# Four-column scaling moved to ScalarE, and GpSimd's value scaling cut in halves, in a chain of attention and two expert layers

## The chip, the cores and the metric

The kernel runs on one core of a Trainium2 chip. A core has five engines that run side by side: TensorE (PE in the profile; its weight loads are PEld) for matrix products, VectorE (DVE), ScalarE (ACT), GpSimd (POOL), and SyncE (SP), which here issues all DMA transfers. Each works through its own queue in order. The metric is the device time of one execution in microseconds, the median over several; lower is better.

## What is computed

```python
# q, k, v: 4 batches x 8 heads x 576 positions x 64
scores = where(block(i) >= block(j), q @ k.T / 8, -1e9)      # blocks of 64 positions
x = softmax(scores) @ v                                      # to 2304 tokens x 512
p = domain_probs / (domain_probs.sum(-1) + 1e-9)             # 2304 x 4
y = sum over e of p[:, e:e+1] * (relu(x @ w1[e]) @ w2[e])    # 4 experts, 512 -> 1024 -> 512
h = y @ w_in                                                 # 512 -> 1024
s = h * softmax(h)
out = (s - mean(s)) / sqrt(var(s) + 1e-6) * g_ln @ w_out     # 1024 -> 512
```

## The kernel before

The 2304 tokens are 18 tiles of 128 rows. Products run in 16-bit pieces: a tensor is scaled by a power of two, its high part is the value rounded to 16 bits, its low part what remains, and three products of the parts stand for one. So nearly every operand is made in two instructions: a high part on ScalarE or GpSimd, then a low part on VectorE that reads it.

The attention goes batch by batch and tile by tile. The values of a batch are five blocks of 128 x 512 (the first batch is key 0; two more blocks, whose key is a tuple, serve the first query block of two batches each). For the second to fourth batch a block is loaded, its squares are summed for the scale, it is loaded again when its turn comes (vraw), and v_split makes its parts: the high part on GpSimd (line 881), the low part on VectorE (line 882). The product of probabilities and values is line 1021; the probabilities come to it transposed, pT, through a DMA.

When the attention of a tile is ready, finish() closes it in three steps: rows (divide by the sums), scale (sum of squares, from which scale_bits on VectorE computes a power of two, inv, and its reciprocal s), and split: the high part on ScalarE (line 1074), the low part on VectorE (line 1075), a transposing DMA to xT, which the expert layers read, and the tile's four expert probabilities pn multiplied by inv into pt, 128 x 4 numbers (line 1079).

coef_of reads pt on VectorE and multiplies in the scales of the weights: for one tile at a time where an expert's result opens the accumulator (line 454, used on ScalarE at line 417), and for a whole part of the tiles at once else (line 460, used by line 422). Tiles 0 to 5 are the first part, 6 to 17 the second.

The expert layers are units that are mixed in between the steps of the attention: hidden units (line 375 for the products, 385 and 386 for the parts of the result) and output units (line 397). Tiles 0 to 5 go through the first experts while the attention of the others runs. When the attention ends, t_steps and s_steps prepare sums of parts of x and of the weights for the next stage, which needs fewer products (line 629). Weights w_in and w_out come as 64-bit words and are narrowed on VectorE (lines 287 to 310) in between.

The start is emitted in an order written out by hand; there SP's queue is held to the order of emission. Else the program is built with a scheduler that plays a simulated timeline and picks, for each engine, among what is ready by priority; results that TensorE waits for are given a higher one. So an engine's order may differ from the order in the code.

Of the kernel before, what the change touches and what calls it, by code (L numbers as in the profile page):

```python
# [14 lines left out]
AF = mybir.ActivationFunctionType  # L15
ALU = mybir.AluOpType
# [47 lines left out]
def tile_kernel(  # L64
# [38 lines left out]
    vec, act, gp, sync = nc.vector, nc.scalar, nc.gpsimd, InOrder(nc.sync)  # L103
# [18 lines left out]
    pn = cp.tile([128, NTILE, E], F32, name="pn")  # L122
    pt = cp.tile([128, NTILE, E], F32, name="pt")
# [4 lines left out]
    def squares(x, out, junk=None):  # L128

        if junk is None:  # L130
            junk = jp.tile([128, 1024], BF16, tag="junk", name="junk")[:, :x.shape[1]]
        return act.activation(out=junk, in_=x, func=AF.Square, accum_out=out)

    def scale_bits(T, bits, s, inv):

        vec.tensor_scalar(
            out=inv.bitcast(I32), in0=T.bitcast(I32), scalar1=24, scalar2=23,
            op0=ALU.logical_shift_right, op1=ALU.logical_shift_left,
        )
        vec.tensor_scalar(  # L140
            out=inv, in0=inv, scalar1=2.0 ** (64 - bits), scalar2=2.0 ** -75, op0=ALU.mult, op1=ALU.max
        )
        vec.reciprocal(out=s, in_=inv)
# [197 lines left out]
    def xtile(d, t, name):  # L341
        g, c = group(t)
        if g not in d:
            n = GROUPS[g[0]][g[1]][1]
            d[g] = xps[g[0]].tile([128, 2 * KD, 128 * n], F16, tag=f"xT{g[1]}", name=name)
        return d[g][:, :, c:c + 128]
# [397 lines left out]
    class Attention:  # L744
# [132 lines left out]
        def v_split(self, key, j):  # L877
            r = self.raws["v", key, j].pop(0)
            t = self.vp.tile([128, 2, 512], F16, tag="v", name="v")
            s = self.vSc[key]  # L880
            gp.tensor_scalar(out=t[:, 0], in0=r, scalar1=s, scalar2=1.0, op0=ALU.mult, op1=ALU.mult)
            vec.scalar_tensor_tensor(out=t[:, 1], in0=r, scalar=s, in1=t[:, 0], op0=ALU.mult, op1=ALU.subtract)
            self.vS[key, j] = t

# [160 lines left out]
        def finish(self, t):  # L1045

            b, i = TILES[t]
            inv = sp.tile([128, 1], F32, tag="xi", name="xi")
            xf = self.fp.tile([128, NH, HD], F32, tag="xf", name="xf")
            x = xf.rearrange("p h d -> p (h d)")  # L1050
            xh = self.fp.tile([128, 2, 512], F16, tag="xh", name="xh")
            s = sp.tile([128, 1], F32, tag="xs", name="xs")

            def rows():
                ps, sums = self.xps.pop(t), self.sums.pop(t)
                rs = sp.tile([128, NH, 1], F32, tag="rs", name="rs")
                vec.tensor_scalar(
                    out=rs[:, :, 0], in0=sums, scalar1=1e-9 * 2.0 ** PBITS, scalar2=self.vSc[("z", b) if i == 0 else b],
                    op0=ALU.add, op1=ALU.mult,
                )  # L1060
                ri = sp.tile([128, NH, 1], F32, tag="ri", name="ri")
                vec.reciprocal(out=ri, in_=rs)
                vec.tensor_tensor(
                    out=xf, in0=ps.rearrange("p (h d) -> p h d", h=NH), in1=ri.to_broadcast([128, NH, HD]),
                    op=ALU.mult,
                )

            def scale():
                T = sp.tile([128, 1], F32, tag="xt", name="xt")
                squares(x, T, xh[:, 1].bitcast(BF16))  # L1070
                scale_bits(T, 4, s, inv)

            def split():
                act.activation(out=xh[:, 0], in_=x, func=AF.Copy, scale=s)
                vec.scalar_tensor_tensor(
                    out=xh[:, 1], in0=x, scalar=s, in1=xh[:, 0], op0=ALU.mult, op1=ALU.subtract
                )
                sync.dma_start_transpose(out=xtile(xT, t, "xT"), in_=xh.rearrange("p a f -> p (a f)"))
                vec.tensor_scalar_mul(pt[:, t, :], pn[:, t, :], inv)

            return [rows, scale, split]

# [297 lines left out]
    while at1.more:  # L1380
        t, u, cost = moe[-1] if moe else (-1, None, 0)
        ok = t is None or t in ready and len(bg) <= n1
        if not ok or tdv <= tpe + 2.0:
            flush()
            at1.step()
            a, c = at1.cost()
# [233 lines left out]
```

## Time and profile before

| what | value |
|---|---|
| time, median of 3 runs | 1090.99 us (1089.95 to 1091.23) |
| profiled execution, its time | 1090.29 us |
| its span, first to last instruction | 1088.5 us |
| mean granted clock of TensorE, as a share of full | 0.997 |
| TensorE busy | 1041.5 us, 96% of the span |
| VectorE busy | 776.3 us, 71% |
| ScalarE busy | 511.1 us, 47% |
| GpSimd busy | 208.1 us, 19%, all of it before 430 us |
| chain that ended last, by engine | TensorE 84%, DMA 6%, VectorE 4%, GpSimd 3%, ScalarE 1% |

The table is from one execution recorded by the hardware profiler. Busy is the time in which an engine had an instruction under way. The chain that ended last is followed back from the last instruction, at each step to what released it. In the rows below, a window gives its stretch, its length, and for each engine the busy time with the number of instructions in brackets; a timeline gives the start and the duration in us, and in square brackets how long the engine stood idle before and what ended it; a group gives the busy time and the mean of one in ns. An average over the span says little by itself: the kernel has stages with different limits, and the rows below are by stage.

### The profile page before, as it was taken

The page shows a single profiled execution, that of the slowest core. Times are in us where ns is not written, and L with a number is a line of the kernel's source. Part 1 is how long each engine was busy: PE and PEld are TensorE (multiplying, and loading weights), DVE is VectorE, ACT ScalarE, POOL GpSimd, SP SyncE. Part 2 cuts the span into 40 slices and gives each one's busy share as a digit, 9 for nine tenths or more (in the row PEclk, how much of TensorE's full clock was granted, in tenths as well). Part 3 has the DMA queues.
Part 4 walks back from the last instruction along what each step waited for, and adds up shares of the span by engine and source line. Part 5 has one row for each costly group of instructions (what it writes and reads, how often), then busy time and mean ns, then how long its engine had stood idle before and what let it go on. Part 6 is the DMA issues. An engine that isn't in the chain of part 4 may idle for free.

```text
span 1088.5 us, 20680 instructions
## 1 busy us (share of the span) xinstructions
PE 1041.5 (96%) x8088; PEld 657.0 (60%) x8088; DVE 776.3 (71%) x1758; ACT 511.1 (47%) x1108; POOL 208.1 (19%) x280
## 2 busy tenths in 40 slices
PE   4679899999999999999899999999999999999998
PEld 4556666656655655655476777776766674444444
DVE  6879677748767765545786557665879558999883
ACT  5757578546755454532353334231446353323322
POOL 4967733534237311000000000000000000000000
PEclk9989999999999999999999999999999999999999
DMA  9978997566677865235331211330346312435233
GB/s 295 277 175 167 241 201 189 143 173 172 158 178 174 186 112 129 56 90 157 122 97 51 77 47 55 117 136 30 98 145 167 77 24 36 88 88 106 60 87 87
DMA packets 225745, 137.96 MB, mean 127 GB/s; under 512 B 184560, under 2 KB 193008, under 8 KB 225648
## 3 DMA queue, kind: packets, MB, share of 16 engines
q1 hardware_dynamic: 225648, 136.65, 50.3%
q8 instruction: 63, 1.03, 0.4%
q14 instruction: 34, 0.28, 0.1%
HBM read 79.47 MB, written 12.06 MB: 84 GB/s over the span
## 4 chain that ended last, share of the span: by engine, by line
PE 84%; DMA 6%; DVE 4%; POOL 3%; ACT 1%; issue 1%; SPq 0%; DVEq 0%; ACTq 0%; POOLq 0%
PE ops L397 31%; PE hps L629 14%; PE hps L375 14%; PE o L1536 9%; PE h L1470 9%; PE pv L1021 3%; DMA pT<-hl 3%; PE sps L920 2%; PE sps L923 2%; DMA xT<-xh 1%; POOL ks L800 1%; DMA raw<-in_w_dram 1%; DMA x2T<-xh 1%; DMA near<-in_kT_dram 1%; DMA vraw<-in_vC_dram 1%
## 5 line engine op out<-in xcount | busy, mean ns | idle before, releaser
L397 PE MATMUL ops<-wt,hch 128*128 128x512 f16 x1728 | 393.1, 379 | 2.4 <-DVE wt L238 1.4
L397 PEld LDWEIGHTS <-hch 128*128 128x128 f16 x1728 | 166.1, 98 | 187.4 <-issue 6.7
L375 PE MATMUL hps<-xT,wt 128*128 128x384 f16 (+1 forms) x1536 | 216.1, 290 | 6.3 <-DVE hch L386 3.9
L375 PEld LDWEIGHTS <-wt 128*128 128x128 f16 x1536 | 126.5, 100 | 64.4 <-issue 6.1
L979 ACT ACTIVATE p<-sps,nm 128x320 f32<-128x320 f32 (+3 forms) x120 | 70.1, 587 | 85.1 <-DVE nm L939 75.4
L993 DVE TENSOR_TENSOR hl<-p,hl 128x320 f16<-128x320 f32 (+3 forms) x120 | 75.6, 650 | 37.3 <-ACT hl L992 37.2
L629 PEld LDWEIGHTS <-S 128*128 128x128 f16 x1152 | 96.0, 98 | 3.0 <-issue 0.9
L1536 PE MATMUL o<-wt,lt 128*128 128x512 f16 (+1 forms) x456 | 95.6, 368 | 0.0
L1470 PE MATMUL h<-wt,x2T 128*128 128x512 f16 x432 | 95.5, 379 | 0.0
L238 DVE SCALAR_TENSOR_TENSOR wt<-stage,ws,wt 128x1024 f16<-128x1024 f32 (+1 forms) x64 | 82.9, 1304 | 7.4 <-ACT wt L235 4.3
L422 DVE SCALAR_TENSOR_TENSOR acc<-ops,coef,acc 128x512 f32<-128x512 f32 x54 | 40.4, 748 | 66.4 <-PE ops L397 66.3
L920 PE MATMUL sps<-ks,qhi 128*128 128x288 f32 (+3 forms) x160 | 69.1, 433 | 10.7 <-DVE hl L993 7.5
L629 PE MATMUL hps<-T,S 128*128 128x192 f16 x864 | 76.3, 246 | 0.0
L629 PEld LDWEIGHTS <-wt 128*128 128x128 f16 x864 | 72.8, 98 | 5.8
L642 ACT ACTIVATE stu<-hps 128x384 f32<-128x384 f32 x72 | 34.6, 482 | 86.5 <-PE hps L629 86.3
L1536 PEld LDWEIGHTS <-lt 128*128 128x128 f16 x456 | 44.6, 98 | 48.9
L1470 PEld LDWEIGHTS <-x2T 128*128 128x128 f16 x432 | 42.3, 98 | 51.0
L386 DVE SCALAR_TENSOR_TENSOR hch<-hps,hch 128x384 f16<-128x384 f32 (+1 forms) x98 | 52.8, 540 | 21.9 <-ACT hch L385 21.8
L647 ACT ACTIVATE hch<-stc 128x384 f16<-128x384 f32 x72 | 37.4, 521 | 63.5 <-DVE stc L655 63.2
L385 ACT ACTIVATE hch<-hps 128x384 f16<-128x384 f32 (+1 forms) x98 | 46.9, 481 | 39.5 <-PE hps L375 39.4
L1021 PE MATMUL pv<-v,pT 128*128 128x64 f16 x1392 | 56.6, 196 | 8.9 <-DMA pT<-hl 8.8
L1021 PEld LDWEIGHTS <-pT 128*128 128x128 f16 x1392 | 51.6, 100 | 20.5 <-DMA pT<-hl 10.8
(163 smaller groups left out, 1534.6 us busy)
## 6 DMA issues: line engine op xcount, KB each, us to landing
stage<-in_w_dram SPq DMA_DIRECT2D x50, 512.0 KB, 5.9
raw<-in_qT_dram SPq DMA_DIRECT2D x34, 256.0 KB, 3.1
vraw<-in_vC_dram SPq DMA_DIRECT2D x30, 256.0 KB, 3.2
raw<-in_kT_dram SPq DMA_DIRECT2D x24, 288.0 KB, 3.5
raw<-in_w_dram SPq DMA_DIRECT2D x24, 256.0 KB, 4.1
raw<-in_w_in_dram SPq DMA_DIRECT2D x8, 512.0 KB, 4.7
raw<-in_w_out_dram SPq DMA_DIRECT2D x8, 512.0 KB, 4.2
stage<-wf SPq DMA_DIRECT2D x8, 512.0 KB, 6.6
```

The source lines that it names most:

```text
L238: stage["last"] = vec.scalar_tensor_tensor(out=lo, in0=r, scalar=stage[key, "s"], in1=hi, op0=ALU.mult, op1=ALU.subtract)
L375: pe.matmul(ps[:, j * n:j * n + n], w[:, a, kk, f * 128:(f + 1) * 128], x[:, b * KD + kk, c0:c0 + n], start=(m == 0), stop=(m == 3 * KD - 1),)
L385: marks["A"] = nc.scalar.activation(out=h[:, 0, :n], in_=ps[:, :n], func=AF.Relu)
L386: marks["D"] = nc.vector.scalar_tensor_tensor(out=h[:, 1, :n], in0=ps[:, :n], scalar=0.0, in1=h[:, 0, :n], op0=ALU.max, op1=ALU.subtract)
L397: pe.matmul(ps, hch[f][:, a, o0:o0 + 128], w[:, b, f, :], start=(m == 0), stop=(m == 3 * KF - 1))
L629: i = pe.matmul(ps[x][:, jj * HT:jj * HT + HT], lhs(a, kk, jj), rhs(b, kk), start=start, stop=(m == 5), skip_group_check=not first or jj > 0,)
L920: pe.matmul(o, q, rhs, start=True, stop=False)
L979: act.activation(out=src if direct else dst, in_=src, func=AF.Exp, bias=nm[:, j + x:j + x + 1], scale=SCALE, accum_out=sums[:, h:h + 1],)
L993: anc["D"] = vec.tensor_tensor(out=lo, in0=pf, in1=hi, op=ALU.subtract)
L1021: pe.matmul(o, tt[:, a * nch + c, :], v[:, bb, hs], start=(m == 0), stop=(m == total - 1))
L1470: pe.matmul(ps[:, half], x[:, a * KD + kk, c:c + 128], w[:, b, kk, half * 512:half * 512 + 512], start=(m == 0), stop=(m == 3 * KD - 1),)
L1536: pe.matmul(ps, tt[:, x * KF + f], w[:, y, f, c], start=(m == 0), stop=(m == 3 * KF - 1))
```

## The change

In finish(), the multiplication of the four probabilities by inv moves from VectorE to ScalarE, as a copying activation with inv as its scale; its place in the emitted order stays, behind the tile's transposing DMA. In v_split(), GpSimd's high part of a value block is made by two instructions of 256 columns in place of one of 512, for the batches after the first; the first batch and the two blocks with tuple keys keep the one instruction. VectorE's low part stays one instruction of 512 columns.

```diff
@@ v_split
             s = self.vSc[key]
-            gp.tensor_scalar(out=t[:, 0], in0=r, scalar1=s, scalar2=1.0, op0=ALU.mult, op1=ALU.mult)
+            for c in [slice(0, 512)] if isinstance(key, tuple) or key == 0 else [slice(0, 256), slice(256, 512)]:
+                gp.tensor_scalar(out=t[:, 0, c], in0=r[:, c], scalar1=s, scalar2=1.0, op0=ALU.mult, op1=ALU.mult)
             vec.scalar_tensor_tensor(out=t[:, 1], in0=r, scalar=s, in1=t[:, 0], op0=ALU.mult, op1=ALU.subtract)
@@ finish, split
                 sync.dma_start_transpose(out=xtile(xT, t, "xT"), in_=xh.rearrange("p a f -> p (a f)"))
-                vec.tensor_scalar_mul(pt[:, t, :], pn[:, t, :], inv)
+                act.activation(out=pt[:, t, :], in_=pn[:, t, :], func=AF.Copy, scale=inv)
```

## Rows read from the trace of the kernel before

**Rows 1.** Windows: PE, PEld, DVE, ACT, POOL busy us, clock, DMA share, GB/s.
```profile
0.00:165.00 165.00, 126.14 (x1444) 100.02 (x1444) 127.34 (x293) 109.06 (x298) 108.49 (x138) 0.98 0.94 227
165.00:486.00 321.00, 320.60 (x2564) 190.45 (x2564) 213.58 (x453) 184.86 (x429) 99.58 (x142) 1.00 0.62 144
486.00:523.00 37.00, 33.12 (x216) 18.58 (x215) 22.34 (x51) 11.95 (x23) 0.00 (x0) 1.00 0.51 156
```

**Rows 2.** Waits of PE from 0 to 165 us: total us, times, longest.
```profile
PE pv L1021 <- DMA pT<-hl: 8.8, 6, 2.3
...
PE hps L375 <- DMA xT<-xh: 2.3, 2, 1.9
```

**Rows 3.** Waits of PE from 486 to 523 us.
```profile
PE hps L375 <- DVE hch L386: 3.9, 1, 3.9
```

**Rows 4.** Line 1079: ns min/median/max, first and last start, forms.
```profile
L1079 DVE TENSOR_SCALAR pt<-pn,xi x18: 203/243/729, 37.1 to 493.4; 128x4 f32<-128x4 f32 x18
```

**Rows 5.** Groups of DVE by form: busy us, mean ns, idle before.
```profile
L1079 DVE TENSOR_SCALAR pt<-pn,xi 128x4 f32<-128x4 f32 x18 | 6.7, 372 | 0.0
```

**Rows 6.** Timeline of DVE from 64 us: start, duration, instruction, idle before.
```profile
70.33 0.69 DVE L1079 TENSOR_SCALAR pt<-pn,xi 128x4 f32<-128x4 f32 x1
...
71.72 0.75 DVE L1075 SCALAR_TENSOR_TENSOR xh<-xf,xs,xh 128x512 f16<-128x512 f32 x1 [0.39 <-ACT xh L1074]
```

**Rows 7.** Timeline of POOL from 66 us.
```profile
70.01 0.99 POOL L800 TENSOR_TENSOR ks<-raw,ks 64x384 fp32r<-64x384 f32 x1
```

**Rows 8.** Timeline of DVE from 128 us.
```profile
141.85 0.36 DVE L1079 TENSOR_SCALAR pt<-pn,xi 128x4 f32<-128x4 f32 x1
...
144.15 1.17 DVE L882 SCALAR_TENSOR_TENSOR v<-vraw,vs,v 128x512 f16<-128x512 f32 x1 [0.82 <-POOL v L881]
...
145.43 0.74 DVE L1075 SCALAR_TENSOR_TENSOR xh<-xf,xs,xh 128x512 f16<-128x512 f32 x1
...
152.94 0.49 DVE L993 TENSOR_TENSOR hl<-p,hl 128x320 f16<-128x320 f32 x1 [0.36 <-ACT hl L992]
```

**Rows 9.** Timeline of SP's queue from 100 us.
```profile
114.91 7.10 SPq L94 DMA_TRANSPOSE pT<-hl  x1
```

**Rows 10.** Windows of 20 us, columns as in rows 1.
```profile
80.00:100.00 20.00, 20.00 (x284) 15.62 (x282) 17.55 (x39) 16.40 (x38) 11.86 (x16) 1.00 0.85 184
```

**Rows 11.** Timeline of DVE from 30 us.
```profile
37.11 0.21 DVE L1079 TENSOR_SCALAR pt<-pn,xi 128x4 f32<-128x4 f32 x1
...
51.10 0.27 DVE L1079 TENSOR_SCALAR pt<-pn,xi 128x4 f32<-128x4 f32 x1
```

**Rows 12.** Groups of ACT by form: busy us, mean ns, idle before.
```profile
L1538 ACT ACTIVATE o2s<-o,osc 128x512 f32<-128x512 f32 x17 | 11.6, 684 | 32.4 <-PE o L1536 22.3 <-issue 10.1
...
L1538 ACT ACTIVATE o2s<-o,osc 128x256 f32<-128x256 f32 x2 | 0.9, 474 | 4.0 <-PE o L1536 4.0
```

**Rows 13.** Timeline of all engines from 486 us.
```profile
489.93 0.49 ACT L385 ACTIVATE hch<-hps 128x384 f16<-128x384 f32 x1 [2.33 <-PE hps L375]
...
493.02 0.72 ACT L1074 ACTIVATE xh<-xf,xs 128x512 f16<-128x512 f32 x1 [0.65 <-DVE xs L143]
...
493.36 0.22 DVE L1079 TENSOR_SCALAR pt<-pn,xi 128x4 f32<-128x4 f32 x1
...
493.61 0.69 DVE L460 TENSOR_SCALAR coef<-pt,iw 128x12 f32<-128x12 f32 x3
...
494.21 0.75 DVE L1075 SCALAR_TENSOR_TENSOR xh<-xf,xs,xh 128x512 f16<-128x512 f32 x1
```

**Rows 14.** Line 881's instructions, columns as in rows 4.
```profile
L881 POOL TENSOR_SCALAR v<-vraw,vs x15: 687/692/1652, 134.9 to 372.0; 128x512 f16<-128x512 f32 x15
```

**Rows 15.** Line 798's instructions, columns as in rows 4.
```profile
L798 POOL TENSOR_SCALAR qhi<-raw x62: 397/404/1367, 11.8 to 427.7; 128x256 fp32r<-128x256 f32 x56, 128x512 fp32r<-128x512 f32 x6
```

**Rows 16.** Timeline of SP's queue from 134 us.
```profile
143.41 2.33 SPq L94 DMA_TRANSPOSE pT<-hl  x1
...
146.46 1.23 SPq L94 DMA_TRANSPOSE xT<-xh  x1
```

## The prediction

> **What bounds the kernel now.** First the page's busy times, as in the table above: TensorE has an instruction under way for 96% of the span. Only where it has none, or where it does its work slower, can a change to the other engines show. The windows by stage say where that is [rows 1]: from 165 to 486 us TensorE is busy for 320.60 of 321, at a granted clock of 1.00. A microsecond saved on VectorE or lost on GpSimd there changes nothing, because TensorE always has another matrix product to go on with. Idle are 165 - 126.14 = 38.9 us in the first 165 us, where the attention of the first tiles cannot yet feed it, and 37 - 33.12 = 3.9 us between 486 and 523 us, where the attention ends and the next stage begins. (From 523 us on neither edit has an instruction.) Of the waits of TensorE in the first stretch two bear on this change: 8.8 us for the transposed probabilities pT, and 2.3 us for the transposed tiles xT [rows 2]. In the second it is one wait of 3.9 us, for VectorE's line 386 [rows 3]. So the question is what the two edits do in those two stretches.
>
> **What leaves VectorE.** Line 1079 runs eighteen times, 203 ns at the shortest, 243 in the middle, 729 at the longest, the first at 37.1 and the last at 493.4 us [rows 4]; the group of them takes 6.7 us, 372 ns in the mean [rows 5]. Four numbers in each row can't take 729 ns by themselves. The one at 70.33 lasts 0.69 us and so ends at 71.02 [rows 6]; GpSimd's product from 70.01 lasts 0.99 us and ends at 71.00 [rows 7]. The VectorE instruction stood until GpSimd's had finished. [...] Eleven of the eighteen run after 165 us, where TensorE doesn't idle, but for the last. Of the seven before, the one at 70.33 is followed by 0.39 us in which VectorE waits for ScalarE's line 1074 in any case [rows 6], so its 0.69 us are swallowed. That at 141.85 is followed by a wait of 0.82 us for GpSimd's line 881 [rows 8]. Around the one at 110.79 the queue of SP is the late one: its transposes from 114.91 hold it for 7.10 us [rows 9], and what VectorE would give earlier stands in line there. The one at 93.02 lies in a stretch where TensorE was busy throughout [rows 10], and that at 151.44 is followed by another wait of VectorE for ScalarE [rows 8]. Two remain, that at 37.11 (0.21 us) and that at 51.10 (0.27 us) [rows 11], in rows of VectorE work without a gap. Upper bound of the gain 0.5 us, lower bound nothing, if the transposes later take it back; I take 0.2.
>
> **What comes to ScalarE.** The trace has no activation on four columns. The nearest rows are line 1538's, 684 ns for 512 columns and 474 for 256 [rows 12]: 0.82 ns a column, and 684 - 508 x 0.82 = 267 ns for four. Eighteen of them are at most 4.8 us on an engine that is idle for half of the span. Each comes behind line 1074 of its tile, so its operands are there and it waits for nothing itself. Queued behind it are exponentials and high parts of the next step. On a path to TensorE before 165 us that costs between nothing and 0.27 us, once; I take 0.1. [...]
>
> **The wait that it adds.** Lines 454 and 460 read pt on VectorE, and used to follow line 1079 on the same engine. Now they need a signal from ScalarE. For all but one tile there are many microseconds between. The exception is the last tile: pt at 493.36, at once three coefficients of line 460 (0.69 us for the three), then line 1075 at 494.21, and from that the transpose that the next stage waits for; line 1074 of this tile lies at 493.02 and lasts 0.72 us [rows 13]. With pt on ScalarE it is done at about 493.74 + 0.27 = 494.0. If the coefficients stay in front of line 1075, they end at 494.0 + 0.69 = 494.7 and line 1075 is up to 0.5 us later; TensorE's wait of 3.9 us [rows 3] grows by it. If the scheduler puts them behind it, which they allow (their first use is a stage later), line 1075 starts at 493.8, 0.4 us earlier. Bounds -0.4 and +0.5. I take -0.2, the nearer to the second order, since pt is then the operand that comes last.
>
> **The halves.** Line 881 takes 687 ns at the shortest for 512 columns [rows 14]. The nearest row for 256 is line 798's 397 to 404 ns [rows 15]: two halves are 0.80 us, 0.11 us more than one whole, and at the very most, if a half took as long as the whole, 0.69 us more; line 798's row, the same operation at that width, is the near one. Fifteen of them are 1.7 to 10.4 us on GpSimd. From 165 to 486 us it is busy for 99.58 of 321 us [rows 1], so the ten of them that lie there cost nothing. The five of the second batch lie between 134 and 146 us. There the path is: vraw lands, line 881, line 882 of VectorE at 144.15 behind a wait of 0.82 us for it, line 1075 at 145.43 [rows 8], the transpose at 146.46 [rows 16], and TensorE waits 1.9 us for that xT [rows 2]. Line 882 needs both halves. So +0.1 us, at most 0.7; nothing if its place is taken by other work. What the halves could give is a shorter stand for a VectorE instruction behind GpSimd, half of 0.69 us at a time; no VectorE instruction of line 1079's kind is seen standing behind line 881 in front of an idle TensorE, so I put it at nothing and at 0.3 us as the bound.
>
> **The sum.** -0.2 + 0.1 - 0.2 + 0.1 = -0.2 us; with all the bounds at one end -0.5 - 0.4 - 0.3 = -1.2, at the other 0.27 + 0.5 + 0.7 = +1.5. The profiled execution took 1090.29 us, with 1.8 us around its span; the median of the runs is 1090.99, 0.7 above it, and the same difference goes on that: 1090.8, between 1089.8 and 1092.5. A measurement of this kernel tells about 0.2%, 2.2 us, from no change, so that is the same time.
>
> **Rivals.** The order of each engine comes from a scheduler that plays a timeline, so moving eighteen instructions and adding fifteen can turn the order of others round wherever two were ready together.
> First, faster. At 143 us line 1075's operands had been there since ScalarE ended line 1074, and it stood behind line 882, which waited. If the halves, ready later, let line 1075 go ahead, its transpose is no longer late: by 0.6 us if SP still issues the pT transpose of 143.41 first (it holds the queue for 2.33 us), by the whole 1.9 us of TensorE's wait if it doesn't [rows 2, 16]. Together with 0.4 us at the hand-over and the upper bound of 0.5 us for VectorE's relief that is -2.8 us: 1088.2. For it: 38.9 us of idle time, in a stretch where VectorE is busy for 127.34 of 165 us [rows 1]. Against it: most of the seven are swallowed. It decides from 2.2 us on.
> Second, slower: the coefficients' wait. If the scheduler puts pt of the last tile not straight behind line 1074 but behind an activation that waits for TensorE, as line 385 does for 2.33 us at 489.93 [rows 13], VectorE stands at line 460 with line 1075 behind it, and the wait of 3.9 us becomes 6.2: 1090.99 + 2.3 = 1093.3. It decides as soon as pt comes more than 2.2 us behind line 1074. Against it: pt is ready at the same time as line 1074.
> Third, slower: the transposes. They are TensorE's largest wait in the first stretch, 8.8 us in six waits [rows 2], on one queue with the loads. If the order on that queue changes for the worse, one more wait of the size of the longest, 2.3 us, comes in, or two: 1093.3 to 1095.6.
> That the halves or the move don't do what they say is part of the forecast: it is the same time.
>
> **Chances.** The sum as worked out, same time: 0.46. Faster by turned order and relief: 0.32. The coefficients' wait 0.09, the transposes 0.13: slower 0.22. The range goes from 1086.0 (the first rival twice as large) to 1094.5 (the third, between one and two waits), and leaves out about 2 in 10; the likeliest case's own range is 1089.8 to 1092.5.
>
> **What would show it.** Eighteen activations of line 1079 at 0.2 to 0.3 us on ScalarE; thirty instructions of line 881 on loaded values at about 0.4 us; VectorE's busy time some 6 us lower before 494 us; TensorE as full from 165 to 486 us as now, and 38 to 40 us of idle time before that. The step on the hand-over is read at the last line 1075: before 494.21, counted from its line 1074, or after. Wrong I would be if TensorE's idle time in the first 165 us moves by more than 2 us, or its wait near 520 us by more than one.

## The result and the profile after

The changed kernel takes 1096.49 us (median of 8 runs, 1093.15 to 1099.91), the kernel before beside it 1089.65 (8 runs, 1086.23 to 1091.23): a ratio of 1.0064, with a 95% interval of 1.0046 to 1.0082. By the ratio that is 7.0 us slower, above the range of the forecast. The profiled execution of the changed kernel has a span of 1095.0 us, against 1088.5.

First the windows of the changed kernel; the columns are those of [rows 1]. Its source has one line more, so from line 882 on its lines count one higher: its 882 and 1080 are the edited lines 881 and 1079, its 1075 is ScalarE's line 1074 and its 1076 VectorE's line 1075. The prose below goes by the numbers of the kernel before; the lines of a trace have those of their own kernel, and the code cut of r11 and some of the recorded expectations those of the changed one.

```profile
0.00:165.00 165.00, 124.18 (x1407) 100.93 (x1408) 124.49 (x284) 107.38 (x299) 111.23 (x139) 0.96 0.90 223
165.00:486.00 321.00, 317.94 (x2559) 188.22 (x2559) 206.67 (x436) 186.49 (x438) 104.95 (x156) 1.00 0.63 144
486.00:523.00 37.00, 36.55 (x232) 20.27 (x230) 21.59 (x48) 12.46 (x26) 0.00 (x0) 1.00 0.57 166
```

TensorE idles for 165 - 124.18 = 40.8 us in the first stage, 2.0 more than before, and part of what it does there is done at a lower granted clock (0.96 against 0.98). The new thing is in the second row: 321 - 317.94 = 3.1 us without work where it had 0.4 [rows 1]. The third row looks better only because everything comes some 6 us later, and the wait before the next stage has moved past 523 us.

A count of TensorE's progress says where the time goes. It is the start of the matmul of sps (the scores) with n others of sps before it, worked out from the traces (us); the last three columns are experiments told below.

```
   n    before     after      r10      r12      r13
 140    108.72    108.09   107.64   108.67   106.03
 180    130.44    132.72   130.02   132.51   127.86
 220    164.46    168.64   164.38   168.13   165.18
 260    212.78    218.57   214.22   216.08   214.52
 380    348.65    355.14   352.05   351.84   350.75
 495    477.76    484.22   482.97   481.32   480.67
```

At 108 us the changed kernel is 0.6 us ahead. At 130 it is 2.3 behind, at 165 us 4.2, at 213 us 5.8 and at 349 us 6.5, and that stays. The waits of TensorE from 0 to 165 us, against [rows 2]:

```profile
PE pv L1022 <- DMA pT<-hl: 5.9, 3, 3.7
...
PE hps L375 <- DMA xT<-xh: 2.2, 2, 1.6
...
PE pv L1022 <- POOL qlo L800: 1.8, 1, 1.8
```

The transposed probabilities are waited for three times in place of six, 5.9 us in all in place of 8.8, but once for 3.7 us in place of 2.3 at most. The timeline of TensorE shows that place. Before:

```profile
124.08 1.05 PE L1021 MATMUL pv<-v,pT 128*128 128x64 f16 x30 [0.84 <-DMA pT<-hl]
...
129.24 1.05 PE L1021 MATMUL pv<-v,pT 128*128 128x64 f16 x30 [1.89 <-DMA pT<-hl]
...
134.10 1.05 PE L1021 MATMUL pv<-v,pT 128*128 128x64 f16 x30 [0.93 <-DMA pT<-hl]
```

And in the changed kernel:

```profile
123.35 1.04 PE L1022 MATMUL pv<-v,pT 128*128 128x64 f16 x30
128.04 1.78 PE L1022 MATMUL pv<-v,pT 128*128 128x64 f16 x30 [3.65 <-DMA pT<-hl]
129.63 0.51 PE L921 MATMUL sps<-ks,qhi 128*128 128x192 f32 x1
```

Two groups of pv now stand back to back in TensorE's queue, and the second waits 3.65 us with all the sps and hps work behind it that used to lie between them. Behind the wait the same 30 matmuls take 1.78 us and not 1.05. The windows of 10 us (length, TensorE's busy time and instructions, granted clock, DMA share, GB/s) show why, and show it once more behind the waits at 150 us:

```profile
120.00:130.00 10.00, 6.34 (x82) 0.84 1.12 226
130.00:140.00 10.00, 10.00 (x136) 0.82 0.81 183
150.00:160.00 10.00, 7.41 (x95) 0.83 0.92 235
```

Counted from windows of 2 us, the profiled execution of the changed kernel has four stretches at half clock up to its last matmul (a granted clock of 0.50 by windows of 0.5 us, near 74, 130, 156 and 528 us), 17.0 us together, the one of before a single stretch of 6.8 us near 74 us. The mean granted clock of the runs is 0.993 against 0.997.

Now the two edits' own instructions, against [rows 4, 14] (ns min/median/max, first and last start, forms):

```profile
L1080 ACT ACTIVATE pt<-pn,xi x18: 281/296/310, 37.8 to 498.7; 128x4 f32<-128x4 f32 x18
...
L882 POOL TENSOR_SCALAR v<-vraw,vs x30: 475/528/1497, 137.6 to 379.4; 128x256 f16<-128x256 f32 x30
```

Two halves take 1.06 us by the median, where the whole took 0.69. And ScalarE's timeline shows that pt does not stand behind the activation of its tile (line 1074), as in the source, but in front of it:

```profile
144.30 0.30 ACT L1080 ACTIVATE pt<-pn,xi 128x4 f32<-128x4 f32 x1 [2.58 <-DVE xi L140]
...
145.62 0.71 ACT L1075 ACTIVATE xh<-xf,xs 128x512 f16<-128x512 f32 x1
```

ScalarE waits there 2.58 us for the tile's xi; over the eighteen it is 9.6 us in five waits. So the scheduler has turned the order of the engines. Against the kernel before, 262 of VectorE's 1,740 instructions that both have, 148 of ScalarE's 847, 53 of SyncE's 389 and 1,840 of TensorE's 8,072 stand at another place of their queue.

### The profile page after: what moved, and what is told of

The parts are those of the page before. It is cut to its first block, busy times and chain, and to the rows that moved or that the text cites. A ratio compares the mean times of both kernels' runs of the same rounds, so it can differ in the third digit from the quotient of the medians.

```text
span 1095.0 us, 20688 instructions
## 1 busy us (share of the span) xinstructions
PE 1044.8 (95%) x8088; PEld 660.4 (60%) x8088; DVE 770.8 (70%) x1740; ACT 515.0 (47%) x1126; POOL 216.2 (20%) x295
## 4 chain that ended last, share of the span: by engine, by line
PE 82%; DMA 6%; POOL 5%; DVE 4%; issue 2%; ACT 1%; SPq 1%; DVEq 0%; ACTq 0%; POOLq 0%
PE ops L397 31%; PE hps L629 14%; PE hps L375 13%; PE o L1537 9%; PE h L1471 9%; PE pv L1022 3%; DMA pT<-hl 2%; PE sps L921 2%; PE sps L924 1%; POOL v L882 1%; DMA xT<-xh 1%; POOL ks L800 1%; POOL qlo L800 1%; DVE hl L994 1%; SPq L94 1%
## 5 line engine op out<-in xcount | busy, mean ns | idle before, releaser
L375 PE MATMUL hps<-xT,wt 128*128 128x384 f16 (+1 forms) x1536 | 218.7, 293 | 4.7 <-DVE hch L386 2.4
L375 PEld LDWEIGHTS <-wt 128*128 128x128 f16 x1536 | 129.3, 102 | 63.6 <-issue 7.9
L629 PEld LDWEIGHTS <-wt 128*128 128x128 f16 x864 | 73.2, 98 | 6.1 <-issue 0.3
```

Source lines behind the costliest of these rows:

```text
L375: pe.matmul(ps[:, j * n:j * n + n], w[:, a, kk, f * 128:(f + 1) * 128], x[:, b * KD + kk, c0:c0 + n], start=(m == 0), stop=(m == 3 * KD - 1),)
L629: i = pe.matmul(ps[x][:, jj * HT:jj * HT + HT], lhs(a, kk, jj), rhs(b, kk), start=start, stop=(m == 5), skip_group_check=not first or jj > 0,)
```

## The experiments

Three theories stood at the start. A: the new order is what costs. B: the halves cost, on the way of the values into pv. C: pt on ScalarE costs. A fourth, D, came up with the half-clock stretches: the clock costs.

Most runs hold four engines to a given order; GpSimd's order is left to the scheduler. Every instruction is recorded as the source makes it, and the kernel's own helper `after`, which orders two instructions of one engine without a semaphore, chains them:

```diff
+def hold(logs, after):
+    for key, order in PIN.items():          # TensorE, VectorE, ScalarE, SyncE
+        log = logs[key]
+        for x, y in zip(order, order[1:]):
+            after(log[y], log[x])
```

PIN holds the order read from the kernel before ("the old order") or from the changed one ("the new order"). No run here holds the kernel before, unedited, to its own old order; that holding costs little by itself is read from r8, r15 and r16 below, which are held to it and stand within 0.4 us of the kernel before. Each ratio is to runs of the kernel before on the same chip beside them (medians 1089.4 to 1091.6 us); microseconds are the ratio's excess times 1090.

**Order against work.** First both edits in the old order, and the old instructions in the new order.

```diff
-PIN = (none: the scheduler's order)
+PIN = the old order     # r1: lines 881 and 1079 edited
+PIN = the new order     # r2: neither line edited
```

> Both edits, with each engine held to the order of instructions that the kernel before had (each activation of line 1080 right behind its tile's line 1075, as the source has it). Theory A, the order: the 6.8 us come from the order in which the scheduler puts the instructions of VectorE, ScalarE, SyncE and TensorE once the edits are in; then this run stands at 0.0 to +1.5 us against the kernel before (ratio up to 1.0014). Theory B, the halves' own price: two halves take 1.06 us against 0.69, fifteen times, on the values' way into pv of the second batch; then the run stands at +3 to +6 us whatever the order. Theory C, ScalarE's new work: 18 activations of 0.28 us make ScalarE late for what follows; then +2 to +5 us here too.

> The kernel before's own instructions (whole line 881, line 1079 on VectorE) with each engine held to the order that the changed kernel has. Theory A, the order: +4 to +7 us against the kernel before (1094 to 1097 us), with half-clock stretches at about 127 and 154 us as in the changed kernel. Theories B and C: -0.5 to +1.5 us, since neither the halves nor ScalarE's 18 activations are in it.

Measured: r1 1.0036 (1.0022 to 1.0051), +3.9 us; r2 1.0053 (1.0040 to 1.0065), +5.8 us. The order alone, with nothing of the change in it, costs most of what the change costs: theory A holds. But the work in the old order isn't free either, against A's expectation for r1, and the two don't add up (9.7 for 7.0).

**Each edit alone**, first in the scheduler's own order (r3, r4), then in the old one (r5, r6), and both in the old order with pt in front of line 1074 (r7).

```diff
# r3, r6: line 1079 alone
-                vec.tensor_scalar_mul(pt[:, t, :], pn[:, t, :], inv)
+                act.activation(out=pt[:, t, :], in_=pn[:, t, :], func=AF.Copy, scale=inv)
# r4, r5: line 881 alone
-            gp.tensor_scalar(out=t[:, 0], in0=r, ...)
+            for c in ...:
+                gp.tensor_scalar(out=t[:, 0, c], in0=r[:, c], ...)
```

> Only line 1079 on ScalarE, the order left to the scheduler. Theory A, the order: 41 of SyncE's 389 and 116 of ScalarE's 847 instructions change places, so a loss of +1 to +6 us is possible without any halves, and its place in the span is where the waits of pv on pT move. Theory B, the halves' price: 0.0 +- 1 us. Theory C, ScalarE's new work: +3 to +6 us.

> Only line 881 in two halves from the second batch on, the order left to the scheduler (76 of VectorE's and 16 of SyncE's instructions change places). Theory B, the halves' price: +3 to +6 us, with VectorE's line 883 waiting for the halves of 144 to 147 us. Theory A: between 0 and +3 us, the smaller part of the loss, since fewer instructions change places than with line 1079 moved. Theory C: 0.0 +- 1 us.

> Only line 881 in two halves, with VectorE, ScalarE, SyncE and TensorE held to the order of the kernel before. Both edits in this order gave +3.9 us. Theory B, the halves' own price on the values' way into pv: +2 to +4 us here. Theory C, ScalarE's 18 small activations: 0.0 +- 1 us here. The run with the halves alone in the scheduler's own order gave +0.1 us, which speaks for the second.

> Only line 1079 on ScalarE, each activation right behind its tile's line 1074, and the engines held to the order of the kernel before. Theory C, ScalarE's work: an activation of 0.28 us in a row of work that TensorE waits for; +2 to +4 us, with TensorE's waits on p, qhi, hch or hl grown and the VectorE time of 3.9 us that it frees of no use. Theory A, the order alone: 0.0 +- 1 us. Theory B: 0.0 +- 1 us.

> Both edits, held to the order before as in the run with +3.9 us, except that each activation of line 1080 now stands in front of its tile's line 1075, as the changed kernel's own order has it. If ScalarE standing in front of line 1075 for the tile's xi is what costs, this run is 1 to 3 us above that one (+5 to +7 us against before). If the place does not matter, +3 to +5 us, the same as with the activation behind.

Measured: r3 1.0027 (1.0014 to 1.0040), +2.9 us; r4 1.0001 (0.9989 to 1.0012), +0.1; r5 1.0016 (0.9998 to 1.0035), +1.7; r6 1.0031 (1.0016 to 1.0046), +3.4; r7 1.0035 (1.0017 to 1.0054), +3.8. The halves cost nothing that can be told in the one order, and between -0.2 and +3.8 us in the other: theory B is at most a smaller part. Line 1079 on ScalarE costs in either. Its place in front of line 1074 or behind makes no difference in the old order. Of VectorE's waits in r3, one bears on what follows:

```profile
DVE c L454 <- ACT pt L1079: 0.5, 2, 0.4
```

**What of line 1079 costs.** r8 leaves it out, r9 makes each activation twice, both in the old order.

```diff
# r8
-                vec.tensor_scalar_mul(pt[:, t, :], pn[:, t, :], inv)
# ... and lines 454 and 460 read pn in place of pt
# r9
-                vec.tensor_scalar_mul(pt[:, t, :], pn[:, t, :], inv)
+                for _ in range(2):
+                    act.activation(out=pt[:, t, :], in_=pn[:, t, :], func=AF.Copy, scale=inv)
```

> The kernel before in its own order with line 1079 left out on both engines: the coefficients read the probabilities without the row scale (lines 454 and 460 take pn in place of pt). It leaves out that product, so its output is not the reference's. With line 1079 on ScalarE in this order the kernel stood at +3.4 us. Theory C, the 18 activations on ScalarE cost it: -0.5 to +0.8 us here. Rival, VectorE running 3.9 us freer shifts its evictions and so TensorE's waits and its clock: +2 to +4 us here too.

> As the run with line 1079 on ScalarE in the order before (+3.4 us), with each of the 18 activations made twice. Theory C: the price doubles, +5 to +8 us. If the second costs nothing more (+2.5 to +4.5 us), what costs is not ScalarE's time but that VectorE or a wait has shifted.

Measured: r8 0.9997 (0.9984 to 1.0009), -0.3 us; r9 1.0040 (1.0028 to 1.0052), +4.4. VectorE without the eighteen instructions is neither faster nor slower, and twice the time on ScalarE costs about a microsecond more, not another 3.4. So it is hardly the 0.3 us of an activation. That points to something that the first one brings and the second doesn't double, such as a wait. The waits of VectorE from 0 to 165 us in r6 begin with one that the kernel before doesn't have:

```profile
DVE c L454 <- ACT pt L1079: 7.0, 4, 2.5
```

The same in r9:

```profile
DVE c L454 <- ACT pt L1080: 8.4, 4, 2.8
```

Line 454 makes the first expert's coefficient of a tile, in the middle of the attention. VectorE's timeline in the kernel before, around the fifth tile:

```profile
110.79 0.73 DVE L1079 TENSOR_SCALAR pt<-pn,xi 128x4 f32<-128x4 f32 x1
111.55 0.27 DVE L454 TENSOR_SCALAR c<-pt,iw 128x1 f32<-128x1 f32 x1
111.74 0.15 DVE L871 COPY vt<-vtp 128x1 f32<-128x1 f32 x1
```

The coefficient follows its pt at once. In r6 the same place is this, on VectorE:

```profile
109.31 0.16 DVE L143 RECIPROCAL xs<-xi 128x1 f32<-128x1 f32 x1
111.98 0.27 DVE L454 TENSOR_SCALAR c<-pt,iw 128x1 f32<-128x1 f32 x1 [2.51 <-ACT pt L1079]
112.17 0.15 DVE L871 COPY vt<-vtp 128x1 f32<-128x1 f32 x1
```

on ScalarE:

```profile
111.05 0.72 ACT L1074 ACTIVATE xh<-xf,xs 128x512 f16<-128x512 f32 x1
111.66 0.29 ACT L1079 ACTIVATE pt<-pn,xi 128x4 f32<-128x4 f32 x1
```

and on TensorE:

```profile
112.38 1.03 PE L1021 MATMUL pv<-v,pT 128*128 128x64 f16 x30 [0.77 <-DVE vt L871]
```

VectorE has the scale at 109.5 us. Then it stands 2.51 us, because ScalarE has four other activations to do first and reaches pt at 111.66; behind line 454 in VectorE's queue stands vt, and for that TensorE waits. Yet this pv is not later than in the kernel before:

```profile
112.95 1.04 PE L1021 MATMUL pv<-v,pT 128*128 128x64 f16 x30
```

So the line above shows a way to TensorE, but not the 3.4 us. In r3, in the scheduler's own order, line 454 waits 0.5 us in all; what r3 loses is not this wait. The three runs that follow test the wait of line 454: pt on ScalarE for tiles 0 to 6 alone (r14) or 7 to 17 alone (r15), and for all of them with line 454 freed of it (r16), all in the old order.

```diff
# r14: t < 7, r15: t >= 7
+                if t < 7:
+                    act.activation(out=pt[:, t, :], in_=pn[:, t, :], func=AF.Copy, scale=inv)
+                else:
                     vec.tensor_scalar_mul(pt[:, t, :], pn[:, t, :], inv)
# r16: line 1079 on ScalarE as in r6, and line 454
-                out=c, in0=pt[:, t, e:e + 1], scalar1=c1, scalar2=c2, ...
+                out=c, in0=pn[:, t, e:e + 1], scalar1=c1, scalar2=c2, ...
```

> The order before; line 1079 on ScalarE for tiles 0 to 6 alone (those of the first 165 us), on VectorE for the others. All 18 on ScalarE gave +3.4 us, none at all -0.3 us, each of them twice +4.4 us. If ScalarE is late only where TensorE waits for chains through p, hl and pT, that is in the first 165 us: +2.5 to +4 us here. If every tile costs its share: +1.0 to +1.6 us (7 of 18).

> The order before; line 1079 on ScalarE for tiles 7 to 17 alone, after 165 us, where TensorE is full. If ScalarE is late only in the first 165 us: -0.5 to +0.8 us. If every tile costs its share: +1.8 to +2.4 us (11 of 18).

> The order before and line 1079 on ScalarE for all 18 tiles, as in the run with +3.4 us, except that line 454 (the first expert's coefficient, tile by tile in the attention stage) reads the probabilities without the row scale and so waits for nothing of ScalarE's. It leaves out that scale in those coefficients, so its output is not the reference's. In the run with +3.4 us VectorE stood 7.0 us in four waits of line 454 on pt. If these waits are the cause: -0.5 to +1.0 us. If ScalarE's own time is: +2.5 to +4.5 us still.

Measured: r14 1.0032 (1.0018 to 1.0046), +3.5 us; r15 1.0004 (0.9989 to 1.0019), +0.4; r16 1.0003 (0.9984 to 1.0023), +0.3. In r16 the eighteen activations are all there and VectorE's line 454 waits for nothing:

```profile
109.35 0.25 DVE L454 TENSOR_SCALAR c<-pn,iw 128x1 f32<-128x1 f32 x1
109.89 0.16 DVE L871 COPY vt<-vtp 128x1 f32<-128x1 f32 x1 [0.29 <-PE vtp L869]
```

Five runs in the old order have line 454 waiting for pt (r1, r6, r7, r9, r14: 4.6 to 8.4 us in four waits); they stand at +3.4 to +4.4 us. Three don't (r8, r15, r16); they stand at -0.3 to +0.4. Two with the halves and without the wait (r5, and r17 below) stand at +1.7. So theory C holds, but through line 454, which now needs a result of ScalarE, and not as ScalarE's time.

One rival is not ruled out. GpSimd's order was left to the scheduler, and by the traces it turned in just the five runs with the wait, at 12 to 27 of 280 places (two halves counted as one); in r5, r8, r12, r15, r16 and r17 it is that of the kernel before, in r2, r10, r11 and r13 that of the changed one. GpSimd in the kernel before:

```profile
121.03 1.92 POOL L800 TENSOR_TENSOR qlo<-raw,qhi 128x256 fp32r<-128x256 f32 x2
122.93 0.42 POOL L798 TENSOR_SCALAR ks<-raw 128x288 fp32r<-128x288 f32 x1
```

and in r6:

```profile
121.08 1.33 POOL L798 TENSOR_SCALAR ks<-raw 128x288 fp32r<-128x288 f32 x2
122.38 1.42 POOL L800 TENSOR_TENSOR qlo<-raw,qhi 128x256 fp32r<-128x256 f32 x2
```

Freeing line 454 (r16) took away both, so the runs do not separate VectorE's wait from GpSimd's turned order. The clock may have a part as well, by an estimate: over the 118 runs of the kernel before that stand beside the experiments, 0.001 less of mean granted clock goes with some 0.7 us more. The five runs' means are 0.992 to 0.995, against 0.996 to 0.997 for the three and 0.997 for the kernel before; that would be 1 to 3 of their 3.4 to 4.4 us. It is a correlation, and no run tests it. How the 3.4 us come together isn't shown: r6's profiled execution was its fastest, 1090.65 us.

**Where the order costs.** r11 is the changed kernel with the second of the two pv groups put 45 matmuls later in TensorE's queue. r10 leaves the order and fills the two waits with matmuls that pv then writes over.

```diff
# r11: TensorE's part of PIN, instructions by their number in the source's order
-  ..., 893 to 922 (pv of tile 5, pair 2), 45 matmuls of lines 921 to 926, 397 and 375, ...
+  ..., 45 matmuls of lines 921 to 926, 397 and 375, 893 to 922 (pv of tile 5, pair 2), ...
# r10: in front of the group's first matmul, line 1021
+            for _ in range({(5, 2): 60, (7, 0): 30}.get((t, p), 0)):
+                v = self.vS[b, i]
+                pe.matmul(ps[:, p * 128:(p + 1) * 128], v[:, 0, :128], v[:, 0, :128], start=True, stop=True)
```

> The changed kernel in its own order, except that the 30 matmuls of pv of tile 5, pair 2 stand 45 matmuls later in TensorE's queue, behind work that waits for nothing (sps, ops and hps of lines 921 to 926, 397 and 375), as in the order before. Theory A, the order at this place: the wait of 3.65 us at 128 us goes, and with it the half clock behind it; 2 to 4 us under the changed kernel (+3 to +5 us against before). If the loss is spread over the stages and this place is only one sign of it: less than 1 us under it.

> The changed kernel in its own order, with 60 matmuls of 128 columns put in front of pv of tile 5, pair 2 (the wait of 3.65 us at 124.4 to 128.0) and 30 in front of pv of tile 7, pair 0 (the wait of 1.80 us at 151.0); they write the columns that pv then starts afresh. TensorE has work while it waits for pT, the wait itself is as long. Theory D, that TensorE's clock falls behind these waits and the half-clock stretches at 127 to 134 and 154 to 158 us are a good part of the loss: full clock there and 2 to 4 us under the changed kernel (+3 to +5 us against before). If only the waits' length counts: no change from the changed kernel (+6 to +8 us).

Measured: r11 1.0036 (1.0023 to 1.0049), +3.9 us, by the ratios 3.1 below the changed kernel's 7.0; r10 1.0070 (1.0054 to 1.0085), +7.6. TensorE's timeline in r11 from 120 us on:

```profile
123.73 1.05 PE L1022 MATMUL pv<-v,pT 128*128 128x64 f16 x30 [0.47 <-DMA pT<-hl]
127.07 0.33 PE L921 MATMUL sps<-ks,qhi 128*128 128x192 f32 x1 [0.92 <-ACT p L980]
131.18 0.36 PE L921 MATMUL sps<-ks,qhi 128*128 128x192 f32 x1 [2.34 <-POOL ks L800]
149.27 0.64 PE L1022 MATMUL pv<-v,pT 128*128 128x64 f16 x16 [2.46 <-DMA pT<-hl]
```

The wait of 3.65 us is gone and with it the half clock near 128 us, other waits of 0.9 and 2.3 us have come for it, and the net is a gain: this place is a good part of A. r10 has the full clock where the changed kernel had 0.82 to 0.84, and yet it isn't faster. Its windows:

```profile
120.00:130.00 10.00, 9.79 (x156) 1.00 1.11 235
130.00:140.00 10.00, 9.66 (x144) 1.00 1.02 196
150.00:160.00 10.00, 10.00 (x154) 1.00 1.23 187
...
165.00:486.00 321.00, 315.61 (x2532) 1.00 0.64 141
```

The table of progress above shows it too: r10 is level with the kernel before at 165 us, and 5.2 us behind at 478. In the first 165 us its profiled execution is at half clock (0.50) for 3.4 us, that of the changed kernel for 13.7, and at n = 220 it is 4.3 us ahead of it. What the clock gave back there was lost again in the full stage, where TensorE idles 321 - 315.61 = 5.4 us; why is not shown, nor how much of the 7.0 us is due to the changed kernel's 17.0 us at half clock (6.8 before). So theory D holds for the first stage and not for the end: at the full clock the changed kernel still loses all of it.

The last question is the stage. r12 takes the new order up to 165 us and then the old one, r13 the reverse, both with the old instructions.

```diff
-PIN = the new order     # as r2
+PIN = what starts before 165 us in the new order, then the rest in the old order     # r12
+PIN = what starts before 165 us in the old order, then the rest in the new order     # r13
```

> The kernel before's own instructions; up to 165 us of the span each engine in the changed kernel's order, from there on in its own old one. In the new order throughout the same instructions gave +5.8 us. Theory A1, the loss is made in the first stage, where the transposes and GpSimd's splits come late to TensorE: +4 to +6 us. Theory A2, it is made after 165 us, in small waits while TensorE is nearly full and at the hand-over: -1 to +1.5 us.

> The reverse: the kernel before's instructions in their old order up to 165 us of the span, and from there on in the changed kernel's order. Theory A1: 0 to +1.5 us. Theory A2: +4 to +6 us. If the two halves share it, both runs stand at +2 to +4 us.

Measured: r12 1.0035 (1.0020 to 1.0050), +3.8 us; r13 1.0041 (1.0027 to 1.0056), +4.5. Neither A1 nor A2: each half of the order costs about as much, and together (r2, +5.8) less than the sum. The window from 165 to 486 us tells them apart. Of r12:

```profile
165.00:486.00 321.00, 320.50 (x2573) 1.00 0.62 144
```

Of r13:

```profile
165.00:486.00 321.00, 317.85 (x2559) 1.00 0.63 142
```

With the old order in that stage TensorE idles 0.4 to 2.0 us (the kernel before, r1, r5 to r9, r12, r14 to r17), with the new one 3.1 to 5.4 (the changed kernel, r2, r10, r11, r13), whatever came ahead of it. Some of it is to be seen: from 285 to 400 us TensorE has no wait in the kernel before, and in r13 this:

```profile
PE pv L1021 <- DMA pT<-hl: 2.0, 2, 1.3
```

**Without the waits of line 454.** Both edits, with pt on ScalarE for tiles 7 to 17 alone (the edit of r15), in the old order (r17) and in the scheduler's own (r18).

> Both edits, line 1079 on ScalarE for tiles 7 to 17 alone, and the order before. The halves alone in this order gave +1.7 us (0 to 3.8), the late tiles alone +0.4 us. If the loss of the change is the waits of line 454 and the order: +0.5 to +2.5 us, and no version of the change is faster than the kernel before. If something is still missing from that: over +3 us.

> The same edits as in the run beside it (line 1079 on ScalarE for tiles 7 to 17 alone, the halves from the second batch on), the order left to the scheduler, which keeps the old order on TensorE up to its 1,167th matmul, some 138 us. So the long wait of 3.65 us at 128 us does not come. Theory A: between the old order's time and the changed kernel's, +1.5 to +4.5 us, by what the order behind 138 us costs (it cost 4.5 us in the run that took the new order from 165 us on).

Measured: r17 1.0016 (0.9999 to 1.0034), +1.7 us; r18 1.0026 (1.0009 to 1.0043), +2.8 us. In the old order what is left of the change is what the halves alone gave (r5, +1.7). In the scheduler's own order it is a microsecond more, within the intervals of both. No version of the change came out ahead of the kernel before.

## Why the prediction was wrong

**The failed step** is in "What bounds the kernel now": "because TensorE always has another matrix product to go on with". It has one only in the order that the kernel before has. On that ground the sum has no term for a turned order, which stands among the rivals alone. The new order with the old instructions measured +5.8 us (r2), most of the 7.0. The changed kernel's order leaves 3.1 us idle between 165 and 486 us (0.4 before), and r13, with old instructions throughout, 3.2 us.

**The second** is in "The wait that it adds", the sentence "For all but one tile there are many microseconds between". It was put for lines 454 and 460 alike. But line 454 runs straight behind pt for four early tiles, at 111.55 behind 110.79, with vt behind it in VectorE's queue. The step's price for all tiles but the last was nothing; in the old order it measured +3.4 us (r6) and +3.5 (r14), and +0.3 with line 454 freed (r16), whether by the wait itself or by the order of GpSimd that came with it. In the changed kernel line 454 waits 0.5 us in all, so there this step is not what the 7.0 us are made of.

**The rivals.** The third, the order of the transposes, is the nearest to what came, and had a chance of 0.13. Its place was right in part, the first stage and a longer wait for pT. But it looked for the cause in the queue of the transposes, where r11 gets 3.1 us back by moving TensorE's own matmuls, and in all pT is waited for less than before, 5.9 us for 8.8. Its size, one or two waits of 2.3 us, was too small, because it counted one queue and one stage. The order turned on four engines and in both stages. The first rival, faster by turned order, did not come: line 1075's instruction stays behind line 882's, which read the halves, and the transpose that was issued at 146.46 us [rows 16] is issued at 149.31. The second did not come either: pt of the last tile is there early.

**What was right.** VectorE's relief was put at -0.2 us, bounds 0 to -0.5; leaving the work out altogether gave -0.3 (r8, an interval of -1.7 to +1.0), which doesn't contradict it. VectorE's busy time fell by 5.5 us, some 6 were forecast. An activation on four columns was put at 267 ns and takes 281 to 310, 296 by the median. "Each comes behind line 1074 of its tile" and "waits for nothing itself" both failed in the changed kernel, but in the old order the place cost nothing that can be told (r7 against r1). At the hand-over the forecast was -0.2 us, and the changed kernel's timeline shows 500.41 - 499.47 = 0.94 us from the last tile's activation to its low part, against 1.19 [rows 13]:

```profile
498.74 0.30 ACT L1080 ACTIVATE pt<-pn,xi 128x4 f32<-128x4 f32 x1
499.47 0.72 ACT L1075 ACTIVATE xh<-xf,xs 128x512 f16<-128x512 f32 x1 [0.44 <-DVE xs L143]
499.81 0.68 DVE L460 TENSOR_SCALAR coef<-pt,iw 128x12 f32<-128x12 f32 x3
500.41 0.74 DVE L1076 SCALAR_TENSOR_TENSOR xh<-xf,xs,xh 128x512 f16<-128x512 f32 x1
```

That the number fits is luck: the forecast leaned on coefficients placed behind line 1075, and they stand in front of it; they come in time because pt stands in front of line 1074. Of the signs of being wrong, TensorE's idle time in the first 165 us moved by 2.0 us, at the bound, and its wait for line 386 at the hand-over from 3.9 to 2.4 us, beyond the bound and the other way ([rows 3] and, from 486 to 540 us of the changed kernel, this):

```profile
PE hps L375 <- DVE hch L386: 2.4, 1, 2.4
```

**The halves** were put at 0.80 us a pair and take 1.06, so 0.36 us more than the whole and not 0.11; the bound of 0.69 holds. Line 798's instructions at that width were no good measure for these. What that costs the kernel stays open between +0.1 us (r4) and +1.7 (r5, an interval of -0.2 to +3.8).

**What stays open.** Why the two causes don't add up. The wait of line 454 is long in the old order alone (7.0 us in r6) and short in the new one (0.5 us). But r18, where the early tiles' pt stays on VectorE, is at +2.8 us in the scheduler's own order, so the scheduler did not turn the order for that wait alone. Argued and not shown: a TensorE that is already late waits less for what else is late. The changed kernel, 4.2 us late at 165 us, idles 3.1 us in the full stage, and r10, not late there, 5.4. Which instruction of the new order makes pT late between 165 and 486 us was not tried, nor was a run with GpSimd's order held.

## What to carry to other kernels

Before an instruction goes to another engine, read in the queue it leaves what stands right behind it and reads its result, for each time it runs: a reader that stood there without a wait may then hold up all that is queued behind it, here for up to 2.5 us on an instruction of 0.3. Where a scheduler sets the order, the edit is also a new order for every engine; hold the old order, and run the old instructions in the new one, and the two prices come apart. Hold every engine: the one left free here, GpSimd, turned with the edit. The stage in which TensorE was full here, 0.4 us of idle time in 321, was so in that order only: in the new one it idled 3.1 us.

## What the runs showed of the hardware

Half of line 881's product on GpSimd did not take half its time: 528 ns by the median for 256 columns and 692 for 512 [rows 14]. A stretch of half clock (0.50 from 127.0 to 133.5 us, by windows of 0.5 us) began near 127 us, inside the changed kernel's wait of 3.65 us, and none came with the three waits of 0.84, 1.89 and 0.93 us in the kernel before; with matmuls in the wait (r10) the clock stayed at 1.00. And the time of one program spreads by more than the change was worth: the kernel before ran from 1086.20 to 1095.54 us in all these runs, with mean granted clocks from 0.991 to 1.000.
